# Two left-over block products of each pair through a second level of the seven-product scheme, with weight blocks kept in DRAM

## The chip, the cores and the metric

The kernel runs on one core of one Trainium2 chip. TensorE multiplies matrices, VectorE, ScalarE and GpSimd work element by element, and SyncE (SP) issues most DMAs; each engine works through its own queue in order, and semaphores tie them together. The metric is the device time of one execution in microseconds. All times here are microseconds unless marked ns.

## The reference

There are two parts. The first is a cross attention of 8 batches and 8 heads between 512 tokens and 32 states of width 64; the second a feed-forward part with the gate h*cos(h). All inputs are 32-bit floats except the weights, which come as 64-bit floats.

```python
scores = scale * x @ state^T;  a  = softmax(scores);   xread = a  @ state
scores2 = scale * state @ x^T; a2 = softmax(scores2);  sread = a2 @ x
X = concat(xread, sread) per batch -> (8 * 544, 512)
h = X @ w_in            # 512 -> 2048
out = (h * cos(h)) @ w_out   # 2048 -> 512
```

## The kernel before

**Tiles and steps.** The hidden layer is made in tiles of 128 of its 2048 columns by the 512 tokens of a batch: 16 tiles per batch, 128 in all, and then 16 tiles for the 256 states of all batches. One turn of the main loop is a *step*; step s starts tile s. Two batches form a *pair* of 32 steps (steps 0 to 31 are pair 0, and so on to pair 3; steps 128 to 143 are the state steps). r is the step inside a pair. A pair has four phases of eight tiles; tile i of a phase is numbered 0 to 7.

**Hidden layer.** `hidden` (L463) makes a tile from attention weights and projected states by full products (batches 0 and 1, phase 3 of every pair, and the states). `hidden_a` and `hidden_b` (L521, L544) make two tiles at once by a scheme of seven products on halves of 256 tokens; `sums_a` and `sums_b` add the parts on VectorE, and `sw_sums` (L496) prepares the sums of the weights on GpSimd, for the next two tiles. For an even r, `hidden_a(r)` runs at step r-1 and `hidden_b(r)` at step r. Their PSUM space is two banks, so `hidden_b(r)` needs the banks that `sums_a(r)` has read, `hidden_a(r+2)` those that `sums_b(r)` has read, and a tile of `hidden` the bank that gate4 of the tile two before has read.

**Gate.** `gate`, `gate2`, `gate3`, `gate4` (L560 to L575) are ScalarE, VectorE, ScalarE, VectorE in turn; gate4 writes the tile into a slot of `g_all`. Slots come from the front of a list, `g_free`, and are appended when free.

**Output layer.** It treats w_out and the tiles of a pair as 2x2 blocks and forms seven block products (w_out's blocks a11 to a22, their combinations s1 to s4, L70 to L76, made on GpSimd by `blocks` at steps 16 to 33). `output` (L698) runs for the tile of three steps before (LAG); in phases 0, 1 and 2 it adds one tile to one block product, in phase 3 one to each of two, by `product` (L617), two matmuls of 512 columns. The differences of tiles that the products need are made by `minus` (L579) on GpSimd and VectorE. Two products of a pair, p7 (with s3) and p4 (with a22), are left over and run during the next pair's phases 0 to 2, one tile after each output whose i has i % 3 < 2 (L703), and for the last pair one per state step (L760). They gather in the PSUM banks SIDE; L625 adds the result to `pr.u` in a held buffer. `later` is a list of VectorE work (totals, and `store`: a transpose into `ot` and four DMAs on SP), of which one item is taken per step. The end products of the states, `state_products` (L762), come last.

**Attention.** `plan` (L875) places the parts of the next batch's attention at fixed steps: the turning of tokens at s=1 and 2 of a batch, scores at 5, softmax at 6 to 9, reads at 11 and 12; after `reads(1)` of a batch, SP loads the tokens of the batch behind it (16 DMAs of `load_tokens`, L287, and 4 of `load_x`, L115).

Of the kernel before, what the change touches and what calls it, by code (L numbers as in the profile page):

```python
# [21 lines left out]
def kernel(  # L22
# [46 lines left out]
    w_in = consts.tile([P, NK, Dff], F32)  # L69
    w_out = consts.tile([P, 2, NF, HD], F32)  # L70
    a11, a12 = w_out[:, 0, 0:NH], w_out[:, 0, NH:NF]
    a21, a22 = w_out[:, 1, 0:NH], w_out[:, 1, NH:NF]
    s1 = consts.tile([P, NH, HD], F32)
# [3 lines left out]

    NG = 28
    g_all = consts.tile([P, NG, S], F32)
    g_free = list(range(NG))  # L80
    xT = consts.tile([P, NK, S], F32)
# [84 lines left out]
    def out_load(m, f):  # L166
        return w_out[:, m, f:f + 4], w_out_src[:, m, f:f + 4]

# [413 lines left out]

    MAIN, SIDE = 0, 1

    class Pair:
# [9 lines left out]
        def __init__(self, n, before):  # L595
            self.n, self.before, self.b = n, before, {}
            self.left = [(p7, i) for i in range(NH)] + [
                (p4, i) for i in range(NH)]

        def more(self, n):  # L600

            for _ in range(n):
                if self.left:
                    p, i = self.left.pop(0)
                    p(self, i)

# [33 lines left out]

    def total(out, a, b):
        for ch in range(2):
            later.append(lambda ch=ch: nc.vector.tensor_tensor(
                out.t[:, ch], a.t[:, ch], b.t[:, ch], op=ALU.add))

# [27 lines left out]
    def sums2(t):  # L673
        pr, i = t.pair, t.i
        if t.phase == 3:
            minus(pr, pr.b[1, i].g, pr.b[1, i].g, pr.b[0, i].g)

    def free(t):
        g_free.append(t.slot)

    def p7(pr, i):
        last = product(SIDE, s3, pr.b[2, i], i)
        free(pr.b[2, i])
        if last:
            for ch in range(2):
                plus(pr.u, SIDE, ch, pr.u)
            total(pr.p5, pr.u, pr.p5)
            store(2 * pr.n + 1, 1, pr.p5)

    def p4(pr, i):  # L690
        last = product(SIDE, a22, pr.b[1, i], i)
        free(pr.b[1, i])
        if last:
            for ch in range(2):
                plus(pr.u, SIDE, ch, pr.u)
            store(2 * pr.n, 1, pr.u)

    def output(t):  # L698
        if t.pair is None:
            state_output(t)  # L700
            return
        pr, i = t.pair, t.i
        if t.phase < 3 and pr.before and i % 3 < 2:  # L703
            pr.before.more(1)
        if t.phase == 0:
            if product(MAIN, a11, t, i):
                pr.u = Held()
                keep_product(pr.u, MAIN)
        if t.phase == 1:

            bank = MAIN if pr.before else SIDE
            if product(bank, a12, t, i):
                o = Held()
                for ch in range(2):
                    plus(o, bank, ch, pr.u)
                store(2 * pr.n, 0, o)
        if t.phase == 2:
            if product(MAIN, s1, pr.b[0, i], i):
                pr.p5 = Held()
                keep_product(pr.p5, MAIN, pr.n > 0)  # L720
        if t.phase == 3:
            last = product(SIDE, s4, t, i)
            free(t)
            if last:
                o = Held()
                for ch in range(2):
                    plus(o, SIDE, ch, pr.p5)
            product(MAIN, s2, pr.b[0, i], i)
            free(pr.b[0, i])
            if last:  # L730
                for ch in range(2):
                    plus(pr.u, MAIN, ch, pr.u)
                total(o, o, pr.u)
                store(2 * pr.n + 1, 0, o)
# [8 lines left out]
    def state_sums(t):  # L743
# [9 lines left out]
        for o, x1, x2 in ((t1, b1.g[:, R2], b1.g[:, R1]),  # L753
# [3 lines left out]
            nc.vector.tensor_tensor(o, x1, x2, op=ALU.subtract)  # L757

    def state_output(t):
        t.last_pair.more(1)  # L760

    def state_products():  # L762
# [4 lines left out]
        c21, c22 = [ot[:, HD:Dm] for ot in ots]  # L767
        a, u2, u3 = [xT[:, i, 0:HD] for i in range(3)]

        def mul(x, w, b, start):  # L770
            for i in range(NH):
                nc.tensor.matmul(out=x, lhsT=b(i), rhs=w[:, i, :],  # L772
                                 start=(start and i == 0),
                                 stop=(i == NH - 1), skip_group_check=True)
# [25 lines left out]
        plus(u3, x3, a)  # L800
        mul(x2, s3, lambda i: rows_of[i].g[:, R2], False)
        plus(c22, x2, u3)
# [3 lines left out]
        send(1, 0, c12)  # L806
        mul(x2, a22, lambda i: rows_of[i + NH].x[:, R1], False)
        plus(c21, x2, a)
# [140 lines left out]
    def blocks(op, out_, a, b, r):  # L949
# [7 lines left out]
                21: (ALU.subtract, s4, a12, s2, lo),  # L957
                22: (ALU.subtract, s4, a12, s2, hi),
                32: (ALU.subtract, s3, a11, a21, lo),
                33: (ALU.subtract, s3, a11, a21, hi)}  # L960
    LAG = 3

    line = []
    all_tiles = list(tiles())
    for step, t in enumerate(all_tiles):
# [86 lines left out]
        if step in block_at:  # L1052
            blocks(*block_at[step])
        if t.pair is not None:
            sums2(t)
# [36 lines left out]
```

## Time and profile before

| what | value |
|---|---|
| median of 3 runs (lowest, highest) | 759.77 (758.88, 759.89) |
| profiled execution, its own time | 759.83 |
| its span, first to last instruction | 758.0 |
| granted TensorE clock | 0.997 |
| TensorE busy | 747.9, 2928 matmul instructions |
| VectorE, ScalarE, GpSimd busy | 519.9, 313.2, 256.6 |
| chain that ended last | TensorE 92%, VectorE 3% |
| DMA | 41.46 MB, mean 55 GB/s |

A 32-bit product is two matmul instructions in the profile, so `product` shows as four. In the answers of the trace a line has start and length of a group, engine, source line, operation, what it writes and reads (`out<-in`), shapes and count; in brackets the idle time before it and what ended it. PE is TensorE, DVE VectorE, ACT ScalarE, POOL GpSimd, SPq the queue of SP. Matmuls are pipelined: their lengths overlap, and the distance of their starts tells how fast they go.

### The profile page before, as it was taken

To read this page: it belongs to the slowest core of one execution; us is meant where nothing else is said; L and a number is where in the kernel's file an instruction comes from. 1 tells how busy PE (TensorE), PEld (TensorE's weight loads), DVE (VectorE), ACT (ScalarE), POOL (GpSimd) and SP (SyncE) were. 2 spreads that over 40 slices of the span, in tenths; PEclk is the share of its full clock that TensorE was granted. 3 is DMA by queue.
4 is the path that set the end of the run, shared out by engine and by line. 5 is a ranking of instruction groups with operands and counts; after the bars stand their busy time and mean duration, and the time that the engine had idled before them with its cause. 6 is when DMAs were issued, how large, how long until landed. Compare 5 with 4: busy or idle time off the path is not lost.

```text
span 758.0 us, 8557 instructions
## 1 busy us (share of the span) xinstructions
PE 747.9 (99%) x2928; PEld 389.7 (51%) x2928; DVE 519.9 (69%) x883; ACT 313.2 (41%) x522; POOL 256.6 (34%) x265
## 2 busy tenths in 40 slices
PE   8998999999999999999999999999999999999998
PEld 3443443445555554445555554445555554466666
DVE  5778778736886788846886888747877675434630
ACT  3887843533363435333363336432453333212210
POOL 2354278777121212663121113661121126510000
PEclk9999999999999999999999999999999999999999
DMA  8595471060012510160104310350100110101031
GB/s 249 169 277 200 137 105 29 4 108 1 5 23 37 100 23 10 23 117 0 19 11 75 64 29 1 50 90 1 28 1 1 28 29 0 29 0 29 8 48 28
DMA packets 161291, 41.46 MB, mean 55 GB/s; under 512 B 154016, under 2 KB 154528, under 8 KB 161248
## 3 DMA queue, kind: packets, MB, share of 16 engines
q1 hardware_dynamic: 160160, 40.39, 25.3%
q10 hardware_dynamic: 960, 0.39, 0.2%
q8 instruction: 23, 0.38, 0.2%
q14 instruction: 20, 0.16, 0.1%
q0 software_dynamic: 128, 0.13, 0.1%
HBM read 31.98 MB, written 8.91 MB: 54 GB/s over the span
## 4 chain that ended last, share of the span: by engine, by line
PE 92%; DVE 3%; ACT 1%; DMA 1%; POOL 1%; issue 1%; SPq 0%; DVEq 0%; ACTq 0%; POOLq 0%
PE o L619 51%; PE h L466 15%; PE h L509 14%; PE at L314 5%; PE o L772 2%; PE at L404 2%; PE o L314 1%; PE at L772 1%; PE at L387 1%; DMA x_b<-in_x_dram 1%; ACT q L568 0%; DVE i L328 0%; ACT q L562 0%; PE o L840 0%; POOL g_all L581 0%
## 5 line engine op out<-in xcount | busy, mean ns | idle before, releaser
L619 PE MATMUL o<-g_all,w_out 128*128 128x512 f32 x512 | 237.4, 599 | 0.6 <-POOL w_out L237 0.3
L619 PE MATMUL o<-g_all,s 128*128 128x512 f32 x384 | 177.3, 598 | 0.0
L581 POOL TENSOR_TENSOR g_all<-g_all 128x512 f32<-128x512 f32 x89 | 124.7, 1422 | 107.2 <-DVE g_all L575 107.2
L619 PEld LDWEIGHTS o<-g_all,w_out 128*128 128x128 f32 x512 | 93.8, 190 | 108.6 <-issue 102.6
L568 ACT ACTIVATE q<-q,halfpi 128x512 f32<-128x512 f32 (+1 forms) x144 | 100.7, 700 | 91.1 <-DVE q L565 90.9
L619 PEld LDWEIGHTS o<-g_all,s 128*128 128x128 f32 x384 | 70.8, 190 | 88.1 <-issue 84.4
L466 PE MATMUL h<-aT,sw 128*128 128x512 f32 x224 | 106.4, 598 | 2.9 <-DVE g_all L575 2.4
L562 ACT ACTIVATE q<-g_all 128x512 int32<-128x512 f32 x75 | 46.8, 624 | 142.2 <-DVE g_all L555 141.8
L565 DVE TENSOR_TENSOR q<-q,h 128x512 f32<-128x512 int32 (+1 forms) x69 | 42.9, 622 | 81.6 <-ACT q L562 81.5
L562 ACT ACTIVATE q<-h 128x512 int32<-128x512 f32 (+1 forms) x69 | 37.6, 545 | 108.0 <-PE h L466 108.0
L565 DVE TENSOR_TENSOR q<-q,g_all 128x512 f32<-128x512 int32 x75 | 52.9, 705 | 36.0 <-ACT q L562 36.0
L466 PEld LDWEIGHTS h<-aT,sw 128*128 128x128 f32 x224 | 41.9, 190 | 56.6 <-issue 45.7
L504 POOL TENSOR_TENSOR swS<-sw 128x128 f32<-128x128 f32 x35 | 17.6, 502 | 147.6 <-PE h L509 107.3
L575 DVE TENSOR_TENSOR g_all<-g_all,q 128x512 f32<-128x512 f32 x75 | 54.2, 722 | 14.3 <-ACT q L568 14.3
L575 DVE TENSOR_TENSOR g_all<-h,q 128x512 f32<-128x512 f32 (+1 forms) x69 | 42.9, 622 | 22.8 <-ACT q L568 21.9
L504 POOL TENSOR_TENSOR swS<-sw,swS 128x128 f32<-128x128 f32 x35 | 18.3, 523 | 87.1 <-PE h L509 86.7
L509 PEld LDWEIGHTS h<-aT,sw 128*128 128x128 f32 x144 | 27.4, 190 | 34.4 <-issue 28.5
L509 PE MATMUL h<-aS,sw 128*128 128x256 f32 x144 | 43.1, 381 | 0.1
L509 PE MATMUL h<-aT,sw 128*128 128x256 f32 x144 | 42.8, 379 | 0.0
L509 PE MATMUL h<-aS,swS 128*128 128x256 f32 x144 | 42.8, 379 | 0.0
L237 POOL TENSOR_TENSOR w_in<-w_in,s 128x1024 int32<-128x1024 int32 (+1 forms) x10 | 19.3, 1932 | 36.8 <-DVE w_in L232 22.0
L466 PE MATMUL h<-st_all,w_in 128*128 128x256 f32 x128 | 30.2, 379 | 0.0
(109 smaller groups left out, 889.0 us busy)
## 6 DMA issues: line engine op xcount, KB each, us to landing
g_all<-in_moe_w_out_dram SPq DMA_DIRECT2D x8, 1024.0 KB, 5.1
out_dram<-ot SPq DMA_DIRECT2D x128, 64.0 KB, 2.0
g_all<-in_moe_w_in_dram SPq DMA_DIRECT2D x6, 1024.0 KB, 5.3
xT<-in_x_dram SPq DMA_DIRECT2D x96, 64.0 KB, 2.3
x_b<-in_x_dram SPq DMA_DIRECT2D x24, 256.0 KB, 4.6
x_b<-in_x_dram SPq DMA_DIRECT2D x16, 128.0 KB, 4.0
g_all<-in_moe_w_in_dram SPq DMA_DIRECT2D x4, 512.0 KB, 6.0
s<-in_state_dram SPq DMA_DIRECT2D x8, 32.0 KB, 7.3
```

Source lines behind the costliest of these rows:

```text
L237: nc.gpsimd.tensor_tensor(bits, bits, e, op=ALU.add)
L314: nc.tensor.matmul(out=(to or at)[j][Ns * k:Ns * k + Ns, 0:n], lhsT=w[D * j:D * j + D, self.b, Ns * k:Ns * k + Ns], rhs=r(slice(D * j, D * ...
L466: nc.tensor.matmul(out=t.hp, lhsT=t.lhs(i), rhs=t.rhs(i), start=(i == 0), stop=(i == t.kn - 1))
L504: engine.tensor_tensor(o, x1, x2, op=op)
L509: nc.tensor.matmul(out=out, lhsT=w, rhs=r, start=True, stop=True)
L562: nc.scalar.activation(t.q.bitcast(I32), t.hp, func=ACTF.Copy, bias=0.25)
L565: nc.vector.tensor_tensor(t.q, t.q.bitcast(I32), t.hp, op=ALU.subtract)
L568: nc.scalar.activation(t.q, t.q, func=ACTF.Sin, bias=halfpi, scale=-TWO_PI)
L575: nc.vector.tensor_tensor(t.g, t.hp, t.q, op=ALU.mult)
L581: engine.tensor_tensor(out, a, b, op=ALU.subtract)
L619: nc.tensor.matmul(out=acc[bank][ch], lhsT=w[:, i, P * ch:P * ch + P], rhs=g.g, start=(i == 0), stop=(i == NH - 1))
L772: nc.tensor.matmul(out=x, lhsT=b(i), rhs=w[:, i, :], start=(start and i == 0), stop=(i == NH - 1), skip_group_check=True)
```

## The change

The products p7 and p4 are no longer run tile by tile. Each is a product of a 1024x256 weight block with eight tiles of 512 tokens; it is cut once more into 2x2 and made by seven products (`Inner`), each a *stage* of four matmuls of 128x128 by 256 columns. Both together are 14 stages for one pair, in the place of 16 tile products.

- The weights of the stages, 2 x 8 blocks of 128x512, are made once: `inner_weights` takes four of them as they are, makes four sums (those of a22 on VectorE at step 17, those of s3 on GpSimd at step 22), and writes all eight to DRAM. For that s3 is made on VectorE at steps 20 and 21, no longer on GpSimd at 32 and 33.
- The memory that a21 and a22 had becomes four more slots of `g_all` and a ring of three blocks; after each stage `fetch_block` asks for the block two stages ahead (SP). The end products get four blocks of each from DRAM, by `load_end_weights` at step 128, into `x_b` and `xT`.
- The differences of the tiles are made on GpSimd: `first_sums` at r = 1 and 2, `second_sums` at r = 3, `third_sums` behind stage 2 for p7, and at 11, 12, 13 and behind the third stage of p4; in the state steps at 1, 2, 3 and 7, 8, 9.
- Stage 0 of each is copied by ScalarE to the second bank; each other stage ends with one VectorE addition of 256 columns to `pr.u`. The sum of p5 (`last7`) moves from two VectorE operations in `later` to one of GpSimd, directly behind stage 6.
- After output i of phases 0 to 2, stages run until `(phase * 8 + i + 1) * 7 // 9` are done; in the state steps one per step.

```diff
-    w_out = consts.tile([P, 2, NF, HD], F32)
-    a11, a12 = w_out[:, 0, 0:NH], w_out[:, 0, NH:NF]
-    a21, a22 = w_out[:, 1, 0:NH], w_out[:, 1, NH:NF]
+    NG, NX = 28, 4
+    g_all = consts.tile([P, NG + 2 * NX, S], F32)
+    g_free = list(range(NG))
+    w_0 = consts.tile([P, NF, HD], F32)
+    w_out = [w_0, g_all[:, NG:NG + 2 * NX].rearrange("p t (u d) -> p (t u) d",
+                                                     d=HD)]
+    a11, a12 = w_out[0][:, 0:NH], w_out[0][:, NH:NF]
+    a21, a22 = w_out[1][:, 0:NH], w_out[1][:, NH:NF]
     s1 = consts.tile([P, NH, HD], F32)
     s2 = consts.tile([P, NH, HD], F32)
     s3 = a21
-    NG = 28
-    g_all = consts.tile([P, NG, S], F32)
-    g_free = list(range(NG))
+    NR, NQ = 3, NH // 2
+    ring = [g_all[:, NG + NX + i].rearrange("p (i d) -> p i d", d=P)
+            for i in range(NR)]
+    spare = ctx.enter_context(tc.tile_pool(name="spare", bufs=1,
+                                           space=bass.MemoryType.DRAM))
+    blocks_kept = spare.tile([2, 8, P, NQ * P], F32)
...
         def __init__(self, n, before):
             self.n, self.before, self.b = n, before, {}
-            self.left = [(p7, i) for i in range(NH)] + [
-                (p4, i) for i in range(NH)]
+            self.done, self.inner, self.waiting = 0, None, 0
+            all_pairs.append(self)
         def more(self, n):
-            for _ in range(n):
-                if self.left:
-                    p, i = self.left.pop(0)
-                    p(self, i)
+            while self.done < min(n, 2 * len(ORDER)):
+                which, k = divmod(self.done, len(ORDER))
+                self.done += 1
+                self.inner[which].stage(k)
+                fetch_block(self.n * 2 * len(ORDER) + self.done + NR - 2)
...
-    def total(out, a, b):
-        for ch in range(2):
-            later.append(lambda ch=ch: nc.vector.tensor_tensor(
-                out.t[:, ch], a.t[:, ch], b.t[:, ch], op=ALU.add))
+    def total(out, a, b, pr):
+        pr.waiting = 2
+        def go(ch):
+            nc.vector.tensor_tensor(out.t[:, ch], a.t[:, ch], b.t[:, ch],
+                                    op=ALU.add)
+            pr.waiting -= 1
+        later.extend([lambda: go(0), lambda: go(1)])
...
         if t.phase == 3:
             minus(pr, pr.b[1, i].g, pr.b[1, i].g, pr.b[0, i].g)
+            if i == NH - 1:
+                pr.inner = [Inner(pr, 0, last7), Inner(pr, 1, last4)]
...
-    def p7(pr, i):
-        last = product(SIDE, s3, pr.b[2, i], i)
-        free(pr.b[2, i])
-        if last:
-            for ch in range(2):
-                plus(pr.u, SIDE, ch, pr.u)
-            total(pr.p5, pr.u, pr.p5)
-            store(2 * pr.n + 1, 1, pr.p5)
-
-    def p4(pr, i):
-        last = product(SIDE, a22, pr.b[1, i], i)
-        free(pr.b[1, i])
-        if last:
-            for ch in range(2):
-                plus(pr.u, SIDE, ch, pr.u)
-            store(2 * pr.n, 1, pr.u)
+    ORDER = (0, 5, 1, 6, 4, 3, 2)
+    def quarters(m):
+        m = m.rearrange("p (k i) (m d) -> p m k i d", k=2, m=2)
+        return m[:, 0, 0], m[:, 0, 1], m[:, 1, 0], m[:, 1, 1]
+    def inner_weights(which, m, engine):
+        m11, m12, m21, m22 = quarters(m)
+        slots = [g_free.pop(0) for _ in range(4)]
+        t1, t2, t3, t4 = [g_all[:, n].rearrange("p (i d) -> p i d", d=P)
+                          for n in slots]
+        for o, x1, x2, op in ((t1, m21, m22, ALU.add),
+                              (t2, t1, m11, ALU.subtract),
+                              (t3, m11, m21, ALU.subtract),
+                              (t4, m12, t2, ALU.subtract)):
+            engine.tensor_tensor(o, x1, x2, op=op)
+        for n, block in enumerate((m11, m12, t4, m22, t1, t2, t3, m21)):
+            nc.sync.dma_start(
+                out=blocks_kept[which, n].rearrange("p (i d) -> p i d", d=P),
+                in_=block)
+        g_free.extend(slots)
+    def fetch_block(n):
+        if n < B * len(ORDER):
+            which, k = divmod(n % (2 * len(ORDER)), len(ORDER))
+            nc.sync.dma_start(
+                out=ring[n % NR].rearrange("p i d -> p (i d)"),
+                in_=blocks_kept[which, ORDER[k]])
+    class Inner:
+        def __init__(self, pr, which, last):
+            self.pr, self.which, self.last = pr, which, last
+            tiles = [pr.b[2 - which, i] for i in range(NH)]
+            self.low, self.high = tiles[0:NQ], tiles[NQ:NH]
+            banks = acc[SIDE][which], acc[SIDE][1 - which]
+            self.x1, self.x3 = banks[0][:, LO], banks[0][:, HI]
+            self.x2 = banks[1][:, HI if which else LO]
+        def begin(self):
+            self.slots = [g_free.pop(0) for _ in range(NQ)]
+            self.t1 = [g_all[:, n, LO] for n in self.slots]
+            self.t2 = [g_all[:, n, HI] for n in self.slots]
+        def differ(self, o, x1, x2):
+            nc.gpsimd.tensor_tensor(o, x1, x2, op=ALU.subtract)
+        def first_sums(self, i):
+            lo, hi = self.low[i].g, self.high[i].g
+            self.differ(self.t1[i], lo[:, HI], lo[:, LO])
+            self.differ(self.t2[i], hi[:, HI], self.t1[i])
+        def second_sums(self):
+            for lo, hi in zip(self.low, self.high):
+                self.differ(lo.g[:, HI], hi.g[:, HI], lo.g[:, HI])
+        def third_sums(self):
+            for t2, hi in zip(self.t2, self.high):
+                self.differ(t2, hi.g[:, LO], t2)
+        def stage(self, k):
+            pr = self.pr
+            n = (pr.n * 2 + self.which) * len(ORDER) + k
+            x, b, start, q = (
+                (self.x1, [t.g[:, LO] for t in self.low], True, None),
+                (self.x2, self.t2, False, (0, HI)),
+                (self.x1, [t.g[:, LO] for t in self.high], False, (0, LO)),
+                (self.x2, [t.g[:, HI] for t in self.low], False, (1, HI)),
+                (self.x3, self.t1, True, (1, HI)),
+                (self.x2, self.t2, False, (1, LO)),
+                (self.x3, [t.g[:, HI] for t in self.high], False, (0, HI)),
+            )[k]
+            for i in range(NQ):
+                nc.tensor.matmul(out=x, lhsT=ring[n % NR][:, i], rhs=b[i],
+                                 start=(start and i == 0), stop=(i == NQ - 1),
+                                 skip_group_check=True)
+            if q is None:
+                nc.scalar.copy(self.x2, x)
+            else:
+                while pr.waiting:
+                    later.pop(0)()
+                o = pr.u.t[:, q[0], q[1]]
+                nc.vector.scalar_tensor_tensor(out=o, in0=x, scalar=TWO_PI,
+                                               in1=o, op0=ALU.mult,
+                                               op1=ALU.add)
+            if k == 2:
+                self.third_sums()
+            if k == 3:
+                for t in self.low:
+                    free(t)
+            if k == 5:
+                g_free.extend(self.slots)
+            if k == 6:
+                for t in self.high:
+                    free(t)
+                self.last(pr)
+    def last7(pr):
+        nc.gpsimd.tensor_tensor(pr.p5.t, pr.u.t, pr.p5.t, op=ALU.add)
+        pr.u.done()
+        store(2 * pr.n + 1, 1, pr.p5)
+    def last4(pr):
+        store(2 * pr.n, 1, pr.u)
...
         pr, i = t.pair, t.i
-        if t.phase < 3 and pr.before and i % 3 < 2:
-            pr.before.more(1)
+        if t.phase < 3 and pr.before:
+            pr.before.more((t.phase * NH + i + 1) * 7 // 9)
...
+    end_weights = [x_b.rearrange("p c h d -> p (c h d)"),
+                   xT.rearrange("p k s -> p (k s)")]
+    def load_end_weights():
+        for which, v in enumerate(end_weights):
+            for i, n in enumerate((0, 1, 7, 3)):
+                nc.sync.dma_start(out=v[:, NQ * P * i:NQ * P * i + NQ * P],
+                                  in_=blocks_kept[which, n])
     def state_output(t):
-        t.last_pair.more(1)
...
-        a, u2, u3 = [xT[:, i, 0:HD] for i in range(3)]
+        a, u2, u3 = [g_all[:, g_free.pop(0), 0:HD] for _ in range(3)]
+        v3, v22 = [v.rearrange("p (m k i d) -> p m k i d", m=2, k=2, d=P)
+                   for v in end_weights]
...
             for i in range(NH):
-                nc.tensor.matmul(out=x, lhsT=b(i), rhs=w[:, i, :],
+                rhs = (w[:, i, :] if len(w.shape) == 3 else
+                       w[:, :, i // NQ, i % NQ, :])
+                nc.tensor.matmul(out=x, lhsT=b(i), rhs=rhs,
...
         plus(u3, x3, a)
-        mul(x2, s3, lambda i: rows_of[i].g[:, R2], False)
+        mul(x2, v3, lambda i: rows_of[i].g[:, R2], False)
...
         send(1, 0, c12)
-        mul(x2, a22, lambda i: rows_of[i + NH].x[:, R1], False)
+        mul(x2, v22, lambda i: rows_of[i + NH].x[:, R1], False)
...
                 21: (ALU.subtract, s4, a12, s2, lo),
-                22: (ALU.subtract, s4, a12, s2, hi),
-                32: (ALU.subtract, s3, a11, a21, lo),
-                33: (ALU.subtract, s3, a11, a21, hi)}
+                22: (ALU.subtract, s4, a12, s2, hi)}
...
+    def inner_steps(step):
+        n, r = divmod(step - 2 * NF, 2 * NF)
+        if step < 2 * NF or not all_pairs[n].inner:
+            return
+        for inner, at_ in zip(all_pairs[n].inner,
+                              ((1, 2, 3), (11, 12, 13)) if n < B // 2 - 1 else
+                              ((1, 2, 3), (7, 8, 9))):
+            if r == at_[0]:
+                inner.begin()
+            if r in at_[0:2]:
+                i = 2 * (r - at_[0])
+                inner.first_sums(i)
+                inner.first_sums(i + 1)
+            if r == at_[2]:
+                inner.second_sums()
...
+        if step == 17:
+            inner_weights(1, a22, nc.vector)
+        if step in (20, 21):
+            r = (lo, hi)[step - 20]
+            nc.vector.tensor_tensor(s3[:, r], a11[:, r], a21[:, r],
+                                    op=ALU.subtract)
+        if step == 22:
+            inner_weights(0, s3, nc.gpsimd)
+            g_free.extend(range(NG, NG + NX))
+        if step == 28:
+            fetch_block(0)
+            fetch_block(1)
+        if step == B * NF:
+            load_end_weights()
+        inner_steps(step)
```

## The prediction

> **What bounds the kernel now.** I read the page's busy row first, then the matmul groups with what ended the idle time before them, then the timelines of TensorE and VectorE side by side around each place that the change touches. "r" is the step inside a pair, 0 to 31, as in the description above.
>
> ```profile
> PE 747.9 (99%) x2928; PEld 389.7 (51%) x2928; DVE 519.9 (69%) x883; ACT 313.2 (41%) x522; POOL 256.6 (34%) x265
> ...
> L619 PE MATMUL o<-g_all,w_out 128*128 128x512 f32 x512 | 237.4, 599 | 0.6 <-POOL w_out L237 0.3
> ```
>
> TensorE never rests, and almost nothing ends an idle time before it. That looks as if every matmul removed were won. Three lines later it doesn't. First, pair 1 at r=3 and r=4 (TensorE, then VectorE; columns are start, length):
>
> ```profile
> 192.07 3.61 PE L619 MATMUL o<-g_all,w_out 128*128 128x512 f32 x8
> 195.52 0.59 PE L509 MATMUL h<-aT,sw 128*128 128x256 f32 x2
> 196.07 0.67 PE L509 MATMUL h<-aT,swS 128*128 128x256 f32 x2
> ...
> 195.24 0.69 DVE L541 TENSOR_TENSOR g_all<-g_all,h 128x512 f32<-128x512 f32 x1
> ```
>
> `hidden_b(4)` should go on at 195.95 and goes on at 196.07, 0.14 after VectorE's last sum of `sums_a(4)` ends (195.93) and gives back the bank. VectorE's queue since 190.65 is full (transposes, four L625, gate2, three sums). So the 3.45 before it, one left-over product and one product, just fill TensorE's time. Second, pair 1 at r=26 and r=27:
>
> ```profile
> 304.55 1.88 PE L466 MATMUL h<-aT,sw 128*128 128x512 f32 x4
> ...
> 308.86 1.88 PE L466 MATMUL h<-aT,sw 128*128 128x512 f32 x4
> ...
> 302.98 0.63 DVE L575 TENSOR_TENSOR g_all<-h,q 128x512 f32<-128x512 f32 x1
> ...
> 307.70 0.68 DVE L575 TENSOR_TENSOR g_all<-h,q 128x512 f32<-128x512 f32 x1
> ```
>
> Tiles 26 and 27 take the banks that gate4 of tiles 24 and 25 frees at 303.61 and 308.38: TensorE has 0.9 and 0.5 in hand. Pair 2 has the same figures 166 later; pair 3 has no next batch to prepare and no such tightness.
>
> [...] The trace agrees: the mean of one is 599 ns, but eight fill 3.45 (192.07 to 195.52), a pitch of 430. I use pitches. [...] The trace agrees: a subtraction L488 takes 1.49 while GpSimd works and 0.41 when it is done.
>
> ```profile
> 315.25 1.49 DVE L488 TENSOR_TENSOR aS<-aT 128x256 f32<-128x256 f32 x1
> ...
> 318.07 0.41 DVE L488 TENSOR_TENSOR aS<-aT 128x256 f32<-128x256 f32 x1
> ```
>
> [...]
>
> **Matmul work.** A left-over product of one tile (p7, p4) is four instructions of 512 columns; a stage is eight of 256. The state steps show both:
>
> ```profile
> 681.29 1.88 PE L619 MATMUL o<-g_all,w_out 128*128 128x512 f32 x4
> 683.01 1.89 PE L466 MATMUL h<-st_all,w_in 128*128 128x256 f32 x8
> 684.73 1.88 PE L619 MATMUL o<-g_all,w_out 128*128 128x512 f32 x4
> ```
>
> 1.72 each; the end's rows of 16 make it 1.73 for eight narrow ones. Per pair 16 x 1.72 = 27.5 becomes 14 x 1.73 = 24.2: -3.3, in four pairs -13.2. What of this arrives depends on where it is taken. The left-over products stood at r=3,4,6,7,9,10,11,12,14,15,17,18,19,20,22,23. The stages, by `(n+1)*7//9` and three steps of lag, stand at r=4,5,6,8,9,10,11,13,14,15,17,18,19,20. So r=3, 22 and 23 lose one each, r=5 gains one, 7 goes to 8 and 12 to 13.
>
> - r=3: TensorE reaches `hidden_b(4)` 1.72 sooner and waits for the same sum at 195.93. Won: 0.
> - From `hidden_b(4)` to r=21, where TensorE is full, 14 stages replace 13 products: 24.2 - 22.4 = +1.9 per pair.
> - r=5 to 8: the stage at r=5 moves `hidden_b(6)`, `hidden_a(8)` and VectorE's work behind them by 1.73. With none at r=7 TensorE is back in time at `hidden_b(8)`, VectorE is not: `sums_a(8)` ended at 215.68, now 215.68 + 1.73 + 0.41 (stage 2's addition) = 217.8, plus 0.14; TensorE wants the bank at 216.65. Wait 1.3; in return the wait of 0.16 before `hidden_b(10)` goes. +1.1. With the line above +3.0 per pair, in three pairs +9.0.
> - r=22, 23: -3.44 for TensorE, but tile 26 can't start before 303.6 + 0.1 and tile 27 before 308.4 + 0.1, since VectorE's and ScalarE's chain from `hidden_b(22)` (two gates, spread, shift, maximum, the exponentials that end at 299.92, sums) has nothing removed. So at most 0.4 is won; I take 0.3, in pairs 1 and 2 -0.6. In pair 3, gate4(24) would be ready at about 628.2 and tile 26 comes at 631.4: all is won, -3.4.
> - State steps: a stage per step as before a product; the two products less are the last before the end products, and their gates are done (the last sums end at 726.3, needed at 728.3). -3.3.
>
> **Other engines.** VectorE: per pair 12 additions of 256 columns (0.42, as L777) for six operations of 512 (0.68): 5.0 for 4.1, counted above where VectorE is late; ScalarE two copies of 0.38, with ScalarE 41% busy: 0. GpSimd: per inner scheme 16 differences of 128x256, between 0.46 (128 columns) and 1.27 (512), I take 0.75, and one sum of 128x1024 (2.36) per pair: 32 x 0.75 + 2.4 = 26, in a queue that is busy 18.1 of 60 between 180 and 240. They stand behind sw_sums, whose next call waits for TensorE anyway: 0. [...] 0.3 at each of the two late places, +0.6 per pair, +1.8 (bounds 0 and 4 x 0.75 x 3 = 9).
>
> **Blocks from DRAM.** [...] One place fails. SP at pair 1, r=12:
>
> ```profile
> 234.42 13.70 SPq L287 DMA_DIRECT2D xT<-in_x_dram  x16
> 248.17 3.04 SPq L115 DMA_DIRECT2D x_b<-in_x_dram  x4
> ```
>
> Its second transfer waits for `reads(1)`, done at 240.22; SP is free at 251.2, 11.0 later. Then come the stores of p5, whose time moves from r=15, 16 to r=12, 13 (last7 at r=11): eight issues of 0.50, 4.0. Only then the block for stage 9, emitted at r=13: 15.0 + 2.6 = 17.6 after `reads(1)`. TensorE gets there after product 1.8, hidden_a 1.7, products 1.2, stage and product 3.45, hidden_b 1.3, again 3.45, hidden_a and a transpose 1.85 = 14.8. Wait 2.8 (2.2 to 4.8 by the landing), at r=15 of pairs 1 and 2: +5.6. Pairs 3 and the state steps load no tokens: 0; the eight end weights (4 us of SP at step 128) are needed 70 us later: 0.
>
> **Making the blocks, steps 17 to 28.** VectorE: 4 x 0.6 at step 17 and 1.2 at steps 20 and 21 in place of GpSimd's blocks of steps 32 and 33; VectorE idles 1.26, 1.57 and 2.16 there before its gates, and TensorE has a step in hand: 0 (4.8 without that cover). GpSimd: four sums of 512 columns at step 22.
>
> ```profile
> 129.91 2.34 POOL L950 TENSOR_TENSOR s<-w_out,s 128x1024 f32<-128x1024 f32 x1
> ...
> 137.74 0.63 DVE L575 TENSOR_TENSOR g_all<-h,q 128x512 f32<-128x512 f32 x1
> ...
> 138.45 1.95 PE L466 MATMUL h<-aT,sw 128*128 128x512 f32 x4
> ```
>
> They run from 132.25 to 137.2 (4 x 1.24). Their slots are 27, 18, 19, 20, taken from a list of six, and go back behind 21: step 24's gate4, at 137.74, writes slot 27, which holds t1. t1's write to DRAM is the fifth; the third waits for t4. Issues at 137.3, 137.8, 138.3, landing 140.9; gate4 ends at 141.6, tile 26, that started right behind it at 138.45, at 141.7. Behind the waiting gate4 stand the sums of the softmax and tile 25's gates, so all moves. +3.2 (2.6 to 5.2).
>
> **Sum.** +9.0 + 1.8 + 5.6 - 0.6 - 3.4 - 3.3 + 3.2 = +12.3. The profiled execution took 759.83 (span 758.0 and 1.8 around it; the median is 759.77): 772.1.
>
> **Rivals.** (a) Faster: TensorE sets the pace everywhere and the -13.2 arrives: 746.6. For it speaks the 99%; against it the two places above. It decides if gate4(24) can be ready 2.5 sooner, which needs the exponentials at 299.92 to move. (b) The DMA waits don't come (blocks and t1 land earlier than SP's order says, or slots differ): 772.1 - 5.6 - 3.2 = 763.3. Against it: SP is one queue in order. (c) Landings of 4.6 as for `x_b` (+2.0 at three places, 6.0) and VectorE held in each of its pure SBUF gates at r=1 to 6 (+2 in each pair, an estimate below the bound of 9): 784 at the far end, 778 with the landings alone. (d) The narrow matmuls don't keep 216 ns, as the group means of 297 (42.8/144) could suggest: 56 x 8 x 0.08 = +36; the state steps speak against it, and I put it into (c).
>
> **Chances.** The sum as worked out, 765 to 778: 0.58. (b), 761.3 to 765: 0.12. (a) wholly or in part, below 758.2: 0.14. Within 0.2% (about what a measurement of this kernel can tell from no change): 0.06. (c) and (d), above 778: 0.10. Range 760 to 779: it leaves out most of (a) and of (c). Slower by over 0.2%: 0.58 + 0.12 + 0.10 = 0.80.
>
> **What would show it.** TensorE idle before L466 at step 26 behind a VectorE gate that waits for a DMA; idle before a stage at r=15 of pairs 1 and 2 that ends with a landing in the ring; waits at `hidden_b(4)` and `hidden_b(8)` behind L541, at tiles 26 and 27 behind L575; stages of 1.73. If TensorE has no such idle time, or tile 26 starts at once, I am wrong towards (a).

## The result, and the profile after

The changed kernel takes 795.81 us (median of 4 runs) against 759.83 beside it, a ratio of 1.048 (1.045 to 1.051). The prediction was 772.1, range 760 to 779: the direction held, the size didn't. The profiled execution took 794.34 with a span of 792.6, 34.5 more than the one of before.

First the page of the changed kernel: the busy row, then groups of matmuls (line, operation, count; busy time and mean ns; idle time before them and who ended it).

```profile
PE 749.6 (95%) x3120; PEld 430.5 (54%) x3120; DVE 550.7 (69%) x913; ACT 316.2 (40%) x530; POOL 367.9 (46%) x399
...
L630 PE MATMUL o<-g_all,w 128*128 128x512 f32 x256 | 122.9, 603 | 5.9 <-DVE held L636 5.6
L776 PE MATMUL o<-g_all 128*128 128x256 f32 x448 | 111.4, 393 | 11.7 <-DMA g_all<-blocks_kept 11.7
...
L475 PE MATMUL h<-aT,sw 128*128 128x512 f32 x224 | 108.6, 609 | 9.6 <-DVE g_all L584 9.1
```

TensorE has fewer columns to do and is busy for 1.7 longer. So two things happened: it now waits (for blocks, for gates, for a bank), and some of its matmuls run slowly. The ledger below sets the start of each step's `hidden` against the same step of before; it is worked out from the two timelines of TensorE.

| stretch | predicted | measured |
|---|---|---|
| first 17 steps | 0 | -1.1 |
| making the blocks, steps 17 to 28 | +3.2 | +10.7 |
| r=4 to 11, three pairs | +10.8 | +12.3 (4.1 each) |
| r=12 to 16, pairs 1 and 2 | +5.6 | +15.1 (6.4 and 8.7) |
| r=21 to 27, pairs 1 and 2 | -0.6 | +2.6 |
| r=22, 23 of pair 3 | -3.4 | -3.2 |
| state steps and end | -3.3 | -1.5 |
| small rest between pairs | 0 | -0.4 |
| sum | +12.3 | +34.5 |

The -1.1 is not the change's: the same wait of 1.95 before tile 11 is followed by slow matmuls in this trace of before and not in this one of after (see the last section).

The places, in the order of the prediction. Timelines have start and length; the bracket is the idle time before and its releaser. Pair 1, r=3 and 4, TensorE and then VectorE:

```profile
203.36 1.98 PE L630 MATMUL o<-g_all,w 128*128 128x512 f32 x4 [1.85 <-DVE held L636]
205.18 0.59 PE L518 MATMUL h<-aT,sw 128*128 128x256 f32 x2
206.27 0.67 PE L518 MATMUL h<-aT,swS 128*128 128x256 f32 x2 [0.49 <-DVE g_all L550]
...
199.76 1.16 DVE L584 TENSOR_TENSOR g_all<-g_all,q 128x512 f32<-128x512 f32 x1 [0.17 <-ACT q L577]
...
201.47 2.44 DVE L636 SCALAR_TENSOR_TENSOR held<-o,held 128x512 f32<-128x512 f32 x4
```

The product that is not there any more at r=3 has become a wait for VectorE, as predicted. Only 0.49 of it stands at the sum that the prediction named (L550, which was L541); 1.85 comes one place earlier, at the bank that L636 reads. A gate (L584) takes 1.16 instead of 0.69. Further on, `hidden_b(8)` waits 0.46 and 0.67 for VectorE's sums, together 1.1 for the 1.3 predicted.

Pair 1, r=12 to 15, SP's queue and then TensorE:

```profile
261.58 3.21 SPq L124 DMA_DIRECT2D x_b<-in_x_dram  x4
264.89 5.13 SPq L671 DMA_DIRECT2D out_dram<-ot  x8
270.06 1.46 SPq L726 DMA_DIRECT2D g_all<-blocks_kept  x3
...
272.99 3.68 PE L776 MATMUL o<-g_all 128*128 128x256 f32 x8 [4.43 <-DMA g_all<-blocks_kept]
```

Tokens, stores, then the block, in the predicted order. The wait is 4.43, not 2.8 (in pair 2 it is 5.43), and the stage behind it takes 3.68 where a stage elsewhere takes 1.9.

Pair 1, r=25 to 27:

```profile
316.71 1.88 PE L475 MATMUL h<-aT,sw 128*128 128x512 f32 x4
320.63 2.62 PE L323 MATMUL at<-w_in,st_all 64*32 64x512 f32 x16 [2.04 <-ACT xT L369]
323.19 2.51 PE L630 MATMUL o<-g_all,s 128*128 128x512 f32 x4
325.53 1.88 PE L475 MATMUL h<-aT,sw 128*128 128x512 f32 x4
```

TensorE comes early, as no stages stand at r=22 and 23, and waits, here not at tile 26 behind a gate: `products(3)` (L323) waits for the exponentials that still read the bank. And again what follows is slow: 2.62 instead of 1.09, 2.51 instead of 1.98.

Steps 17 to 27: VectorE's four sums of a22, GpSimd's four of s3, gate4(24), and tiles 20 and 26 on TensorE:

```profile
107.46 5.90 DVE L715 TENSOR_TENSOR g_all<-g_all 128x512 f32<-128x512 f32 x4
...
107.74 2.80 POOL L1073 TENSOR_TENSOR s<-g_all 128x1024 f32<-128x1024 f32 x1
110.50 1.71 POOL L590 TENSOR_TENSOR g_all<-g_all 128x512 f32<-128x512 f32 x1
115.57 1.27 POOL L590 TENSOR_TENSOR g_all<-g_all 128x512 f32<-128x512 f32 x1 [3.36 <-issue]
...
136.25 5.09 POOL L715 TENSOR_TENSOR g_all<-g_all 128x512 f32<-128x512 f32 x4
...
145.57 0.69 DVE L584 TENSOR_TENSOR g_all<-h,q 128x512 f32<-128x512 f32 x1 [3.78 <-DMA blocks_kept<-g_all]
...
115.49 3.25 PE L475 MATMUL h<-aT,sw 128*128 128x512 f32 x4 [2.26 <-DVE g_all L584]
...
146.31 3.35 PE L475 MATMUL h<-aT,sw 128*128 128x512 f32 x4 [4.42 <-DVE g_all L584]
```

The four sums of a22 take 0.87, 2.72, 1.75 and 0.68, one by one. The two long ones (from 108.36 and 111.01) end 0.5 behind the first two GpSimd lines shown; the last (from 112.68) runs while GpSimd is idle.

And two state steps, with the last wait for a block:

```profile
747.10 1.89 PE L475 MATMUL h<-st_all,w_in 128*128 128x256 f32 x8
750.63 1.99 PE L776 MATMUL o<-g_all 128*128 128x256 f32 x8 [1.63 <-DMA g_all<-blocks_kept]
752.46 1.89 PE L475 MATMUL h<-st_all,w_in 128*128 128x256 f32 x8
```

### The profile page after: what moved, and what is told of

Its sections match the earlier page's. It is cut to its first block, busy times and chain, and to the rows that moved or that the text cites. A ratio compares the mean times of both kernels' runs of the same rounds, so it can differ in the third digit from the quotient of the medians.

```text
span 792.6 us, 9267 instructions
## 1 busy us (share of the span) xinstructions
PE 749.6 (95%) x3120; PEld 430.5 (54%) x3120; DVE 550.7 (69%) x913; ACT 316.2 (40%) x530; POOL 367.9 (46%) x399
## 4 chain that ended last, share of the span: by engine, by line
PE 66%; DVE 18%; issue 4%; ACT 4%; DMA 3%; POOL 3%; SPq 1%; DVEq 0%; ACTq 0%; POOLq 0%
PE o L630 26%; PE h L475 11%; PE h L518 10%; PE o L776 9%; PE at L323 4%; DVE q L574 3%; PE o L895 2%; DVE g_all L584 2%; PE at L413 2%; DMA g_all<-blocks_kept 2%; DVE held L636 1%; DVE g_all L564 1%; ACT q L571 1%; SPq L671 1%; ACT q L577 1%
## 5 line engine op out<-in xcount | busy, mean ns | idle before, releaser
L630 PE MATMUL o<-g_all,w 128*128 128x512 f32 x256 | 122.9, 603 | 5.9 <-DVE held L636 5.6
L776 PE MATMUL o<-g_all 128*128 128x256 f32 x448 | 111.4, 393 | 11.7 <-DMA g_all<-blocks_kept 11.7
L475 PE MATMUL h<-aT,sw 128*128 128x512 f32 x224 | 108.6, 609 | 9.6 <-DVE g_all L584 9.1
L748 POOL TENSOR_TENSOR g_all<-g_all 128x256 f32<-128x256 f32 x128 | 102.8, 827 | 13.9 <-PE o L776 11.4
L776 PEld LDWEIGHTS o<-g_all 128*128 128x128 f32 x448 | 85.1, 195 | 37.3 <-DMA g_all<-blocks_kept 12.6
L574 DVE TENSOR_TENSOR q<-q,h 128x512 f32<-128x512 int32 (+1 forms) x69 | 42.8, 620 | 72.0 <-ACT q L571 71.9
L574 DVE TENSOR_TENSOR q<-q,g_all 128x512 f32<-128x512 int32 x75 | 58.3, 778 | 33.3 <-ACT q L571 33.3
L630 PEld LDWEIGHTS o<-g_all,w 128*128 128x128 f32 x256 | 47.9, 193 | 50.3 <-issue 39.5
L584 DVE TENSOR_TENSOR g_all<-g_all,q 128x512 f32<-128x512 f32 x75 | 55.7, 743 | 14.2 <-ACT q L577 14.2
L584 DVE TENSOR_TENSOR g_all<-h,q 128x512 f32<-128x512 f32 (+1 forms) x69 | 42.9, 621 | 30.0 <-ACT q L577 25.8
```

The costliest lines, as they stand in the source:

```text
L475: nc.tensor.matmul(out=t.hp, lhsT=t.lhs(i), rhs=t.rhs(i), start=(i == 0), stop=(i == t.kn - 1))
L574: nc.vector.tensor_tensor(t.q, t.q.bitcast(I32), t.hp, op=ALU.subtract)
L584: nc.vector.tensor_tensor(t.g, t.hp, t.q, op=ALU.mult)
L630: nc.tensor.matmul(out=acc[bank][ch], lhsT=w[:, i, P * ch:P * ch + P], rhs=g.g, start=(i == 0), stop=(i == NH - 1))
L748: nc.gpsimd.tensor_tensor(o, x1, x2, op=ALU.subtract)
L776: nc.tensor.matmul(out=x, lhsT=ring[n % NR][:, i], rhs=b[i], start=(start and i == 0), stop=(i == NQ - 1), skip_group_check=True)
```

## Experiments: the four places one by one

Each of these four kernels is the changed kernel with one edit; they ran on one chip.

**Order on SP.** The blocks are fetched from ScalarE's DMA queue.

```diff
-            nc.sync.dma_start(
+            nc.scalar.dma_start(
                 out=ring[n % NR].rearrange("p i d -> p (i d)"),
```

> Theory, order on SP: the block for stage 9 is late only because SP issues it behind the token loads and the stores of p5; issued from ScalarE's queue it is asked for when stage 7 is emitted, and both waits at r=15 of pairs 1 and 2 go, with the slow matmuls behind them: 6.4 + 8.65 = 15.0 less, 780.8. Rival, landing: the block is late because the transfers of tokens and stores hold the DMA engines; then it is late from any queue and the time stays within 2 of 795.8. What both leave open: two issues per stage on ScalarE could delay a gate, up to +3 per pair.

Measured: 777.94, ratio to before 1.024 (1.022 to 1.026), 17.9 less. Pair 1, r=15, TensorE:

```profile
269.34 0.27 PE L429 MATMUL at<-ident,sr 128*128 128x128 f32 x1
269.45 1.89 PE L776 MATMUL o<-g_all 128*128 128x256 f32 x8
271.18 1.88 PE L630 MATMUL o<-g_all,w 128*128 128x512 f32 x4
```

No wait, no slow stage. The same 256 KB land in 2.7 from here and in 2.9 from SP, so it wasn't the transfer that was slow. The ledger gives -6.4 and -8.6 at r=15 and -2.4 at two late state steps, which had waited for SP too (1.63 of it above). ScalarE's issues cost nothing that shows.

**Order of the writes.** The four sums are written before the blocks that are only copied.

```diff
-        for n, block in enumerate((m11, m12, t4, m22, t1, t2, t3, m21)):
+        for n, block in ((4, t1), (5, t2), (6, t3), (2, t4), (0, m11),
+                         (1, m12), (3, m22), (7, m21)):
```

> Theory: gate4 of tile 24 waits for the write of t1 to DRAM, because that write is the fifth in order and the third waits for t4. With t1, t2, t3, t4 written first, t1 has landed before the gate is ready: 3.8 of the idle 4.4 before tile 26 goes and with it the slow matmuls behind it (1.7): 5.5 less, 790.3. Rival: GpSimd's four sums themselves hold VectorE's gates back there; then the idle time stays above 2 and the gain is below 2.

Measured: 790.55, ratio 1.041 (1.038 to 1.043), 5.3 less, and 5.3 by the ledger at this place (3.7 of waiting, 1.7 behind it). The gate stands at 143.29 with no wait of its own, and tile 26 follows at once:

```profile
144.04 1.98 PE L475 MATMUL h<-aT,sw 128*128 128x512 f32 x4 [0.76 <-DVE g_all L584]
```

**The sums of a22.** One per step at steps 28 to 31; `inner_weights(1, a22, nc.vector)` at step 17 goes, and the first two blocks are fetched at step 33.

```diff
-        if step == 17:
-            inner_weights(1, a22, nc.vector)
+        if 28 <= step < 32:
+            a22_sum(step - 28)
...
-        if step == 28:
+        if step == 33:
             fetch_block(0)
```

> The four weight sums of a22 stand at steps 28 to 31, one in each, not all at step 17 (their writes and the first two blocks' reads follow later). Theory: at step 17 they take 5.9 of VectorE instead of 2.4 because GpSimd works on its own sums then, and TensorE waits 2.26 at step 20 and runs slowly behind it; moved to where VectorE has time, 4.1 goes: 791.7. Rival: the two halves of s3 at steps 20 and 21 (1.7 and 2.2) are what is late; then under 1.5 goes. If steps 28 to 31 have no room either, up to 4 comes back there.

Measured: 791.52, ratio 1.041 (1.040 to 1.043), 4.3 less. In the ledger -2.4 and -1.7 at steps 19 and 20, where TensorE had waited and then run slowly; at steps 28 to 31 nothing comes back, 0.3 does right after. So it was the four sums at that place, not the halves of s3. At the new places, where GpSimd is idle as they start, each of the four takes 0.68:

```profile
159.15 0.68 DVE L735 TENSOR_TENSOR g_all<-g_all 128x512 f32<-128x512 f32 x1
```

**The places of the stages.**

```diff
-            pr.before.more((t.phase * NH + i + 1) * 7 // 9)
+            if i % 3 < 2:
+                pr.before.more(pr.before.done + 1)
```

> The 14 stages stand where the first 14 left-over products stood (r=3,4,6,7,9,10,11,12,14,15,17,18,19,20). Theory: the loss from r=4 to 10, 4.1 in each of three pairs, comes from the places alone, and goes, 12 less; at r=15 the block is issued ahead of half of p5's stores, 2 less in two pairs. 780. [...]

Measured: 782.97, ratio 1.031 (1.029 to 1.033), 12.8 less than the changed kernel. From the start of pair 1 to r=10 the loss against before is 1.0 where it was 4.3, but r=11 and 12 lose 0.9 more. With the same number of stages done, at r=14, it is 1.9 where it was 4.1, in each of the three pairs. The waits at r=15 shrink to 2.60 and 2.83 (with what is behind them, 7.4 less by the ledger, more than the 4 expected; the wait of 2.83 is not followed by slow matmuls). So somewhat over half of the 4.1 per pair is a matter of places; 1.9 is not.

**All four, and then other places.** The four edits together:

> The four edits (blocks from ScalarE's queue, sums written first, a22's sums at steps 28 to 31, stages at the old places) together. Theory, four separate losses: -17.8, -5.4, -4.7 and, without its part of the wait at r=15, which is gone already, -6.8: 761.1. Rival: the losses cover each other (one wait taken away shows another behind it): 766 or more.

Measured: 763.58, ratio 1.0052 (1.0036 to 1.0069). The four losses are separate: singly they give 40.3, of which 7.4 is the fourth's part of the wait at r=15 that the first takes away too; 32.9 is left, and 32.2 came. This kernel still lost at r=26 what the free r=22 and 23 had won (-3.4, then +4.4, in pair 1). So the 14 stages were put where the old places are except r=12 and 20:

```diff
-            if i % 3 < 2:
+            if i % 3 < 2 and 3 + t.phase * NH + i not in (12, 20):
                 pr.before.more(pr.before.done + 1)
```

> As the four edits together, but the stages left out of the 16 old places are those of r=12 and r=20, and r=22 and 23 keep theirs. Theory: TensorE is the bound at r=12 and 20, where leaving out a stage wins 1.73 each; at r=22 and 23 it isn't, so a stage there costs nothing and fills the wait of r=26. In pairs 1 and 2: 3.4 + 0.8 less each, in pair 3 nothing: 8.4 under the four edits, 752.7, faster than before. Rival: the chain of VectorE and ScalarE from r=20 to 26 is late whatever TensorE does at r=12 and 20; then the time is that of the four edits within 2.

Measured: 760.35, ratio 1.0012 (1.0005 to 1.0019): 3.2 under the four edits, not 8.4. The ledger gives the reason, by place: r=12 left out wins its 1.72 in each pair; at r=20 there is +0.5, -1.0 and +0.5 in the three places behind it, nothing in all: what sets the pace there isn't TensorE, as the rival had it. Pairs 1 and 2 win 2.1 and 1.8 against the four edits; pair 3, expected at nothing, loses 1.4, since there the free r=22 and 23 had been won in full. The wait of r=26 is gone, as expected:

```profile
293.83 1.89 PE L799 MATMUL o<-g_all 128*128 128x256 f32 x8
...
302.51 1.09 PE L323 MATMUL at<-w_in,st_all 64*32 64x512 f32 x16
303.53 1.98 PE L630 MATMUL o<-g_all,s 128*128 128x512 f32 x4
305.44 1.98 PE L475 MATMUL h<-aT,sw 128*128 128x512 f32 x4
```

## Experiments: GpSimd's hold, and the slow matmuls

**GpSimd's differences left out** (other numbers in the tiles, so other values come out). GpSimd's hold is here what VectorE's gates take longer beside them: ahead of `hidden_b(4)` of pair 1 two of them took 1.13 and 1.16 (L574, L584) in the changed kernel, instead of 0.69:

```diff
         def differ(self, o, x1, x2):
-            nc.gpsimd.tensor_tensor(o, x1, x2, op=ALU.subtract)
+            pass
```

> GpSimd's 32 differences of each pair are left out (the tiles hold other numbers; the rest is as in the changed kernel). [...] Rival: it is GpSimd's hold that costs the 4.1 per pair: 783.

Measured: 794.54, ratio 1.046 (1.044 to 1.048), 1.3 less; the intervals overlap, so the times alone don't tell it from no gain. The timeline is clearer: those two gates take 0.69 each, and from r=3 to r=12 of pair 1 it gains 1.1, of which 0.9 is the wait for L636 at r=3 (0.95 instead of 1.85); the later wait for the block takes half of it back (4.95 instead of 4.43). In the kernel with stages at r=22 and 23 nothing takes it back:

> The kernel with stages at r=22 and 23, without GpSimd's 32 differences per pair (other numbers in the tiles, the rest unchanged). [...]

Measured: 754.08, ratio 0.991 (0.988 to 0.994), 6.3 less by the medians (7.9 by the ratios, since the two ran beside different runs of before). From GpSimd's hold 0.9 was expected at `hidden_b(4)` and 1.1 at `hidden_b(12)`, in each of three pairs, 6 in all. The sum is as expected, the places only in part: 0.9 comes at `hidden_b(4)`; the wait of 1.0 behind pair 1's L550, which was put at `hidden_b(12)` and which stands in `hidden_b(10)`, stays; and 1.3 comes in bits of 0.15 to 0.5 between r=14 and 21. So that wait isn't GpSimd's hold. VectorE's own twelve additions of 256 columns per pair are left for it, but no run here takes them away. VectorE's two gates ahead of `hidden_b(4)`, first with the differences, then without:

```profile
188.43 1.14 DVE L574 TENSOR_TENSOR q<-q,g_all 128x512 f32<-128x512 int32 x1 [0.76 <-ACT q L571]
...
190.36 1.16 DVE L584 TENSOR_TENSOR g_all<-g_all,q 128x512 f32<-128x512 f32 x1 [0.17 <-ACT q L577]
```

```profile
190.67 0.69 DVE L574 TENSOR_TENSOR q<-q,g_all 128x512 f32<-128x512 int32 x1 [0.76 <-ACT q L571]
...
192.15 0.69 DVE L584 TENSOR_TENSOR g_all<-g_all,q 128x512 f32<-128x512 f32 x1 [0.17 <-ACT q L577]
```

**The differences moved.** The computation needs them, but not at r=3: all `first_sums` of the first inner scheme go to r=1, `second_sums` to r=5.

```diff
+            if inner.which == 0:
+                if r == 1:
+                    inner.begin()
+                    for i in range(NQ):
+                        inner.first_sums(i)
+                if r == 5:
+                    inner.second_sums()
+                continue
             if r == at_[0]:
```

> As the kernel with stages at r=22 and 23, with the first inner scheme's GpSimd differences moved: all eight of first_sums at r=1, where VectorE has time, and second_sums at r=5 instead of r=3. Theory: GpSimd is then idle while VectorE prepares hidden_b(4); 0.9 less in each of three pairs: 757.6, under the kernel before. Rival: sw_sums, queued on GpSimd behind the longer batch at r=1, come late and TensorE waits for them, 761 or more.

Measured: 756.32, ratio 0.9959 (0.9944 to 0.9973): 3.6 under the kernel before by the medians, 4.0 under the kernel with stages at r=22 and 23. The ledger finds 0.7, 0.9 and 0.9 of it at `hidden_b(4)`, as the theory had it. By the ledger of the profiled execution, from the start of pair 1 to the state steps it is 0.5 behind the kernel before; with the stages at r=22 and 23 alone that was 3.2 behind, without any differences 3.3 ahead. In those three pairs TensorE has 3 x 3.3 = 9.9 less to do, and none of the kernels that compute the result gets any of it. TensorE waits for VectorE instead: 4.5 in all for the sums of L550, where before had no such wait above 0.2, although VectorE is busy for only 132 of the 166 of pair 1. The ledger puts the rest in pieces of 0.1 to 1.1 from r=14 to 28. In this trace the gain is that of the state steps and the end (-3.8), where the last pair's stages stand beside little but gates.

**The slow matmuls.** Does the stage behind the wait run slowly because TensorE stood idle? It is given idle work in the wait: matmuls of constants into a bank that is free then.

```diff
+            for _ in range({9: 8, 23: 10}.get(n, 0)):
+                nc.tensor.matmul(out=at[0], lhsT=ident, rhs=w_in[:, 0, 0:S],
+                                 start=True, stop=True)
             for i in range(NQ):
                 nc.tensor.matmul(out=x, lhsT=ring[n % NR][:, i], rhs=b[i],
```

> TensorE does 8 and 10 idle matmuls of 512 columns (3.5 and 4.3) into a free bank ahead of stage 9 of pairs 1 and 2, inside its wait of 4.4 and 5.4 for the block. Theory: the slow matmuls behind the wait come from the idle time itself: the stage and the product behind it take 1.99 and 1.88 again, 1.7 and 3.0 less: 791.1. Rival: they are slow for what arrives then (the block, the stores), whatever TensorE did ahead: 795.8.

Measured: 796.59, ratio 1.048 (1.047 to 1.050), no gain. My sum was off by two: each such matmul is two instructions in the records, so the filling took 7.03 and 8.75 and outlasted the wait. The stages behind it took 1.89. With half as many:

> As the kernel that fills the wait, with half as many idle matmuls, 4 and 5, since each is two instructions and the 8 and 10 took 7.0 and 8.8, longer than the wait: now 3.5 and 4.3. Theory, idle time makes the matmuls slow: the stage starts when the block lands, as in the changed kernel, and it and the product behind it take 1.9 each instead of 3.7 and 1.9 in pair 1, 3.8 and 3.1 in pair 2: 4.7 less, 791.1. Rival, the clock falls for another reason: 795.8.

Measured: 793.14, ratio 1.042 (1.039 to 1.045), 4.3 less than the changed kernel by the two ratios, whose intervals just touch (2.7 by the medians, beside different runs of before). By the ledger r=15 is 0.7 and 4.0 shorter. Pair 1:

```profile
272.03 3.60 PE L776 MATMUL at<-w_in,ident 128*128 128x512 f32 x8
277.62 1.99 PE L779 MATMUL o<-g_all 128*128 128x256 f32 x8 [1.99 <-DMA g_all<-blocks_kept]
279.45 1.88 PE L630 MATMUL o<-g_all,w 128*128 128x512 f32 x4
```

The block lands 5.4 after TensorE's last work of its own (4.4 in the changed kernel's trace); the stage waits for it as it did there, and stage and product take their normal time. In pair 2 the block comes 1.0 sooner than in that trace. With these differences taken out, the slow stretches that are gone are worth 1.7 and 2.9. In these two kernels none of the four filled waits is followed by slow matmuls. So here it was the idle time that made them slow. The granted clock says the same; stretches of the changed kernel ahead of the wait, behind it and later (busy times of PE, PEld, DVE, ACT and POOL, then the clock, DMA share, GB/s; a transfer's share is counted where it starts), then the same stretch with the wait half filled:

```profile
264.00:268.00 4.00, 4.00 (x16) 2.79 (x15) 3.96 (x6) 0.63 (x1) 3.15 (x4) 1.00 1.31 234
273.00:277.00 4.00, 4.00 (x10) 3.05 (x11) 0.29 (x1) 0.00 (x0) 0.00 (x0) 0.57 0.23 85
277.00:281.00 4.00, 4.00 (x27) 1.94 (x26) 1.24 (x3) 0.50 (x1) 0.88 (x2) 1.00 0.20 66
```

```profile
277.60:281.60 4.00, 3.98 (x14) 2.77 (x15) 0.43 (x1) 0.00 (x0) 0.00 (x0) 1.00 0.40 119
```

In the changed kernel TensorE's work behind the six long waits takes longer by 1.7 at step 20, 1.7 at step 26, 1.7 and 3.0 at r=15, and 2.1 and 2.4 at r=26: 12.6 together. Not all of that is added to the time. At r=26 of pair 2 the same wait is followed in four of the experiments by a granted clock of 1.00; here is the half-filled one:

```profile
499.61 1.75 PE L323 MATMUL at<-w_in,st_all 64*32 64x512 f32 x16 [2.04 <-ACT xT L369]
501.30 1.98 PE L630 MATMUL o<-g_all,s 128*128 128x512 f32 x4
503.87 1.98 PE L475 MATMUL h<-aT,sw 128*128 128x512 f32 x4 [0.59 <-DVE g_all L584]
```

`products(3)` is still 0.7 longer than its 1.09, and tile 26 then waits for its gate, and tile 27 for another 0.20. From r=24 to 28 this comes to 4.1 against before, and the changed kernel loses 4.2 and 4.4 there. So the clock cost 0.1 and 0.3 at r=26. At step 20 it is open: in three of the experiments the wait there is 1.57, without slow matmuls, and TensorE waits another 1.57 at tile 25. As an estimate from these figures, the clock's part of the 34.5 is 6.8 to 8.5, of which 4.7 at r=15.

## Why the prediction was wrong, point by point

- **Price of a stage** (1.73): right; eight matmuls of 256 columns take 1.89 with a pitch of 1.73 in the state steps.
- **r=4 to 11** (+3.0 a pair, and +0.6 for GpSimd's hold): right in place and kind, 4.1 for 3.6. The old places take 2.3 of it away; leaving the differences out takes 1.1, so the hold was priced at half of what it is there. No run shows the 0.3 at each late place from which the +1.8 is made; what was measured is two gates 0.44 and 0.47 longer ahead of `hidden_b(4)` of pair 1 (1.13 and 1.16 for 0.69).
- **The block of stage 9** (2.8 each): right in mechanism, the experiment on ScalarE's queue shows it, and the largest miss in size, 15.1 for 5.6. This is the first step that failed, twice over. The waits were 4.43 and 5.43: p5's eight stores took 5.1, not 4.0, and issue with landing 2.9, not 2.6 (no run shows the 2.6 that the sum uses here and behind gate4(24): blocks landed in 2.9 from SP and 2.7 from ScalarE's queue, the writes to DRAM in 2.8, and in the trace of before stores of 64 KB in 2.0 and `x_b` loads of 256 KB in 4.6); in pair 2, where the wait is 1.0 longer, SP's token loads ahead of them took 14.87, not 13.72. And the slow matmuls behind the waits, 1.7 and 3.0, were no term of the sum at all.
- **gate4(24) behind t1's write** (+3.2): the mechanism was right, and writing t1 first took it away. Of its 6.4 the wait is 4.4, more than the stated 3.2; the slow matmuls behind it, 1.7, were missing.
- **VectorE's sums at step 17 costed at 0**: the second step that failed. The prediction named the cover and its price without it (4.8); 4.15 came. It used 0.6 a sum, and the four took 5.9 together, with GpSimd adding its own arrays at the same time; the idle times of 1.3 to 2.2 that were to cover them are shorter than that. The text quoted such a slowing (1.49 for 0.41) and then gave it only 0.3 at each of two late places in a pair. In the trace the sums beside GpSimd's additions took 2.72 and 1.75, the one with GpSimd idle 0.68 (and the s3 halves took 1.68 and 2.19 where the sum had 1.2). Of the 128x512 gates in the same trace (L574, L584), those with both operands in SBUF take up to 1.22 beside GpSimd and at most 0.69 without it, those that read a PSUM bank at most 0.69 in both cases; but a scaling of one array of 128x2 (L355) also went from 0.17 to 1.67. Why GpSimd slows them is not shown.
- **r=21 to 27** (-0.6): +2.6. TensorE is stopped there, as said, but first by the exponentials that read the bank of `products(3)`, 2.04 in one wait; the gates of tiles 26 and 27 come behind that, 0.59 and 0.20 where the clock stays at full. Of the +2.6, 0.4 is slow matmuls. At full clock the two absent stages win 3.4 in each pair and 4.1 is lost behind them; why it is more than they won, and the 0.4 lost at r=21, is not shown.
- **Pair 3** (-3.4): right, -3.2. **State steps** (-3.3): -1.5, since blocks waited on SP there too (0.5 and 1.9), which was costed at 0.
- **Rivals**: (a) is out; the saving came only at r=22 and 23 of pair 3 and, in part, in the state steps. (b) is out: both DMA waits came. (c) had the right direction, but landings were 2.9, not 4.6, and the hold on VectorE's gates was 1.1 a pair in the changed kernel, not 2 or more. (d) is out for steady work; the group mean of 393 for L776 is raised by the slow stretches.

In short, the order of the work and the places of the waits were mostly right, and the sizes were not: +34.5 for +12.3. Of the 22.2 between them, 9.5 stand at r=15 and 7.5 in steps 17 to 28. Waits on SP were longer than their sums, a wait was taken at its length although slow matmuls could follow it, and one slowing that the prediction had quoted (1.49 for 0.41) was not applied where the work was moved to.

## What to carry to other kernels

Where TensorE sets the pace, add a term behind each new wait of the lengths that cost something here, about 2 us or more: 1.7 and 3.0 of slow work behind the two waits for blocks at r=15. Then ask whether something else stops TensorE right behind it; if so, as at r=26, little of that term is added. When work goes to another engine, ask first what GpSimd does in that moment: of the sums of a22 one took 2.72 beside GpSimd's additions and one 0.68 with GpSimd idle. When data is to be fetched, ask which transfers stand ahead in that queue. Moving the fetch was one line of code here. And matmul time taken away counts only where TensorE doesn't then wait for another engine: of 13.2 us, 3.6 arrived in the best version, in its trace all in the one stretch where VectorE had little to do.

## What the runs showed of the hardware

Behind some of TensorE's waits the granted clock falls. In the 4 us behind the waits of 4.43 and 5.43 for blocks it was 0.57 and 0.50 in the changed kernel's trace, behind the wait of 2.26 at step 20 it was 0.57, and behind the wait of 1.95 before tile 11 it was 0.64 in the trace of before and 1.00 in that of the changed kernel. Over the traces of all 13 kernels here, from 15 us on, waits of 1.0 to 1.86 were never followed by a lower clock; waits of 1.95 to 1.99 in 10 of 17 cases (the wait of 1.95 before tile 11 in 7 of 13 kernels, the same code each time); the waits of 2.04 to 2.06 at r=26 in 12 of 16; the four of 2.26 and 2.27 at step 20 all; of four between 2.51 and 2.83 only the one of 2.60; and the fifteen of 3.99 and more all. What decides it in the mixed cases was not shown. From about 2 us on a wait could have a price here, and whether it had differed from one trace to the next.
